# Storing the Q/K stacks of a sliding-window attention in sixteen-row blocks, with overlapping token tiles

## The chip, the cores and the metric

The kernel runs on one core of a Trainium2 chip. The metric is device time in microseconds (us), from the first to the last instruction of one execution, as the median of a few runs. The engines are PE (TensorE, with its weight-load queue PEld), DVE (VectorE), ACT (ScalarE), POOL (GpSimd) and SP (SyncE, which here issues the DMA transfers).

## The reference

A block of two parts. First comes layer norm, attention with a sliding window, the output projection and the residual; then layer norm, a gated MLP whose gate mixes the tokens (a 2048 x 2048 matrix), and the residual. Tokens S = 2048, width D = 640, 32 heads of Dh = 20. The change touches the attention:

```python
H = 32; Dh = D // H; W = 256
q, k, v = qkv[0], qkv[1], qkv[2]
scores = jnp.einsum("bhqd,bhkd->bhqk", q, k) * (Dh ** -0.5)
mask = (idx[:, None] - idx[None, :] >= 0) & (idx[:, None] - idx[None, :] < W)
scores = jnp.where(mask[None, None], scores, -1e9)
p = _softmax(scores, axis=-1)
o = jnp.einsum("bhqk,bhkd->bhqd", p, v)
```

Each query sees itself and the 255 tokens before it.

## The kernel before

**Stacks.** Q and K are wanted at fp32 accuracy from bf16 matmuls. Each is split into three bf16 parts (`split_qk`, the tile `sg`: rounding, remainder, remainder of that). A score is the sum of six products of a Q part and a K part, and all six are done in one matmul by stacking them on partitions: row 6 d + j holds dimension d of the j-th part pair, so 20 dims x 6 pairs = 120 rows. Rows 120 to 122 of the Q side hold the negated row maximum in three parts, against ones on the K side, so that the score matmul already subtracts the maximum.

A stack is for a group g of 4 heads. It lives in one of three slots (two called `slot...`, one in the storage `xb`, which earlier holds the normalized x). Each slot is two tiles, lower and upper, of [128, 2 sides, 4 heads, tokens]: tokens 0 to 1023 and 1024 to 2047. `tokens()` cuts any range of tokens that crosses 1024 into two pieces, and each piece becomes a matmul (with its weight load) of its own.

**From the Q/K GEMM to the stacks.** `qk_item(m, c)` makes 128 rows of Q/K (8 dims x 16 heads of one side or of both; m 0 to 4 are heads 0 to 15, m 5 to 9 heads 16 to 31) for the 512 tokens of chunk c, in 15 matmuls (L592 to L594). Its results are split (DVE L606, ACT L608, POOL or DVE L610, ACT L615 or POOL L613, POOL L616) and stored by one DMA on SP (L619) to the DRAM tensor `qk_d`, laid out [half of the heads, part, token half, dim of both sides, head, tokens]. `load_stack(g)` (L329) is a generator of 24 DMAs on SP: for each tile, pair j and side, 20 rows that lie six partitions apart. For the first three groups it also sets ones by a POOL memset (L322) over partitions 96 to 127.

**Order.** PE, DVE, ACT and SP follow the order of the code; POOL's order is set by a scheduler. m 0 to 5 come first (24 items, load steps of group 0 after the last four). Then `dense_tail` does m 6 to 9, interleaved with the maxima of the first 18 blocks (`LEAD`), whole 128-query matmuls on L363; the stack of group 1 is loaded from its eighth item on. The attention loop has one step s per block of 128 keys (8 groups x 16 blocks). A step issues, for each of the four heads, `max_item` for block s + 18 (L359, four strips of 32 queries, maximum on DVE L369) and `score_item` for block s (L412, four strips of 32 keys, exponential on ACT L415, masks on POOL L419 and L422), and `pv_item` for block s - 2 (L440); it also advances the load of the stack of the group after next. A max item covers its block and two before; a score item its block and the two after it, on the Q side. Both cross token 1024 in the steps 6 and 7 of each group: max blocks 8 and 9, and score blocks 6 and 7. Once in eight blocks `max_rows` transposes the maxima (L375, DVE L378 and L379, POOL L381 and L382), stores them (L384) and loads them as rows 120 to 122 (L386).

Of the kernel before, what the change touches and what calls it, by code (L numbers as in the profile page):

```python
# [34 lines left out]
def block_kernel(ctx, tc, x, xt, wqk, wv, wo, w_in, wsp, bsp, w_out, out):  # L35
# [16 lines left out]
    qk_d = dram.tile([2, 3, 2, 2 * DH, H // 2, S // 4], F32, name="qk_d")  # L52
# [203 lines left out]
    with ExitStack() as ab:  # L256
# [9 lines left out]
        s0 = [s0.tile([P, 2 * S], F32R, name=f"slot0_{i}") for i in range(2)]  # L266
# [12 lines left out]
        add_slot(2, [h[:, :2 * S] for h in xb])  # L279
# [36 lines left out]
        def load_stack(g):  # L316


            st = slot_w[g % 3]
            if g < 3:  # L320
                for h in st:
                    nc.gpsimd.memset(h[96:P, 1], ONES)  # L322
                    if g == 2:
                        yield
            for b in range(2):
                for j, parts in enumerate(((0, 0), (0, 1), (0, 2), (1, 0), (1, 1), (2, 0))):
                    for a in range(2):
                        src = qk_d[g // 4, parts[a], b, a * DH:(a + 1) * DH, g % 4 * 4:g % 4 * 4 + 4]
                        nc.sync.dma_start(st[b][j:6 * DH:6, a], src)  # L329
                        yield  # L330

        def tokens(st, rows, a, hh, t0, n):

            o = 0
            while o < n:
                c, t = divmod(t0 + o, S // 2)
                w = min(n - o, S // 2 - t)
                yield o, w, st[c][:rows, a, hh, t:t + w]
                o += w

        def one(st, rows, a, hh, t0, n):
            (_, _, x), = tokens(st, rows, a, hh, t0, n)
            return x

        def max_item(g, qb, hh, strips=True):

            st = slot_ap[g % 3]
            ps = s1_tile()
            lo = max(0, qb - 2) * P
            n = (qb + 1) * P - lo  # L350
            keep = mask[:, 384 - n:]
            if strips:
                skip = 32 if qb > 1 else 0
                if skip:
                    n, keep = 288, strip
                for j in range(4):
                    q0 = qb * P + 32 * j
                    for o, w, k in tokens(st, 120, 1, hh, lo + skip * j, n):
                        nc.tensor.matmul(ps[32 * j:32 * j + 32, o:o + w], one(st, 120, 0, hh, q0, 32), k,  # L359
                                         start=True, stop=True, tile_position=(0, 32 * j))  # L360
            else:
                for o, w, k in tokens(st, 120, 1, hh, lo, n):
                    nc.tensor.matmul(ps[:, o:o + w], one(st, 120, 0, hh, qb * P, P), k, start=True, stop=True)  # L363
            b, c = divmod(qb, 8)
            if c == 0 and hh == 0:
                m_cols[g, b] = tmp2.tile([P, 32], F32, tag="mcol", bufs=2, name=f"mcol{g}_{b}")
            junk = tmp2.tile([P, 384], BF16, tag="junk", bufs=2, name=f"junk{g}_{qb}_{hh}")
            c += hh * 8
            nc.vector.tensor_tensor_reduce(out=junk[:, :n], in0=ps[:, :n], in1=keep, scale=1.0,  # L369
                                           scalar=NEG, op0=OP.add, op1=OP.max, accum_out=m_cols[g, b][:, c:c + 1])  # L370

        def max_rows(g, b):
# [13 lines left out]
            nc.sync.dma_start(slot_w[g % 3][b][120:123, 0], rows.rearrange("a (h r) c -> a h (r c)", h=4))  # L386
# [4 lines left out]
        def score_item(u, hh):  # L391
# [14 lines left out]
            for i in range(4):  # L406
                k0 = kb * P + 32 * i
                b, e = 32 * i, min(n, 32 * i + 288)
                if NU - NT < u and 4 * (u - NU + NT - 1) + hh < 6:
                    b, e = 0, n  # L410
                for o, w, q in tokens(st, 123, 0, hh, kb * P + b, e - b):
                    nc.tensor.matmul(ps[32 * i:32 * i + 32, b + o:b + o + w], one(st, 123, 1, hh, k0, 32), q,  # L412
                                     start=True, stop=True, tile_position=(0, 32 * i))
# [51 lines left out]
        if True:  # L465
# [137 lines left out]
            def split_qk(m, c, ps):  # L603
# [10 lines left out]
                else:  # L614
                    nc.scalar.activation(sg[:, 1, :], rest, AF.Copy)  # L615
                nc.gpsimd.tensor_tensor(out=sg[:, 2, :], in0=rest, in1=sg[:, 1, :], op=OP.subtract)  # L616
                T = S // 4
                base = qk_d[m // 5, 0, c // 2, m % 5 * 8, 0, c % 2 * 256:c % 2 * 256 + 256]
                nc.sync.dma_start(bass.AP(tensor=base.tensor, offset=base.offset,  # L619
                                          ap=[[T, P], [2 * 2 * DH * H // 2 * T, 3], [1, 256]]), sg.bitcast(F32))  # L620

# [84 lines left out]
            for n in range(24):  # L706
# [11 lines left out]
                if n >= 20:  # L718
                    for _ in range(3):
                        next(ld0, None)  # L720
            def dense_tail():
                split_wqk(8)
                split_wqk(9)
                for n, (m, c) in enumerate((m, c) for c in range(4) for m in (6, 7, 8, 9)):
# [3 lines left out]
                    if n == 7:  # L728
                        x01.close()
                        s1 = pool(x01, "slot1p", side="right")  # L730
                        add_slot(1, [s1.tile([P, 2 * S], F32R, name=f"slot1_{i}") for i in range(2)])
                    if n >= 7:
                        for _ in range(3):
# [3 lines left out]
            for n in range(12):  # L737
                next(dense, None)
                if n % 5 == 4:
                    for _ in range(3):  # L740
# [12 lines left out]
            assert next(dense, 0) == 0 and next(ld0, 0) == 0  # L753
# [6 lines left out]
        for s in range(NU + 2):  # L760
            if s % NT == 0 and s < 6 * NT:
                ld = load_stack(s // NT + 2)
            for _ in range(1 + s % 2 if s >= NT else 2 * min(s, 1)):
                next(ld, None)
# [798 lines left out]
```

## Time and profile before

| | us |
|---|---|
| Runs | 1104.24, 1104.4 (median), 1109.66 |
| Profiled execution | 1106.78 |
| its span | 1105.1 |
| Q/K GEMM with the first 18 blocks' maxima, from the first max item | 178.4 to 240.4 |
| Attention steps 0 to 111 (seven groups) | 240.9 to 440.3 |
| Last group | 440.3 to about 465 |
| Projection, then the gated MLP | about 465 to the end |

The times in the profile are those of the profiled execution, counted from its first instruction. A window row gives start:end and length, and then for each engine its busy time and the number of instructions. In timeline rows the bracket at the end gives idle time of the engine before the row and what ended it; "issue" is time in which the engine waited for nothing that the profile shows. "x4" joins four instructions to one row. The granted TensorE clock is 1.00 in all windows quoted here.

### The profile page before, as it was taken

The page shows a single profiled execution, that of the slowest core. Times are in us where ns is not written, and L with a number is a line of the kernel's source. Part 1 is how long each engine was busy: PE and PEld are TensorE (multiplying, and loading weights), DVE is VectorE, ACT ScalarE, POOL GpSimd, SP SyncE. Part 2 cuts the span into 40 slices and gives each one's busy share as a digit, 9 for nine tenths or more (in the row PEclk, how much of TensorE's full clock was granted, in tenths as well). Part 3 has the DMA queues.
Part 4 walks back from the last instruction along what each step waited for, and adds up shares of the span by engine and source line. Part 5 has one row for each costly group of instructions (what it writes and reads, how often), then busy time and mean ns, then how long its engine had stood idle before and what let it go on. Part 6 is the DMA issues. An engine that isn't in the chain of part 4 may idle for free.

```text
span 1105.1 us, 28747 instructions
## 1 busy us (share of the span) xinstructions
PE 1075.2 (97%) x11059; PEld 968.4 (88%) x11059; DVE 781.0 (71%) x2157; ACT 604.7 (55%) x1258; POOL 314.0 (28%) x447
## 2 busy tenths in 40 slices
PE   8999999999999999999999999999999999999998
PEld 8998886658888787699999998999999899999998
DVE  6643445779999897575677668655556899987684
ACT  4443443249999899756766556443458433333331
POOL 4324446677766666721200012000001000000000
PEclk9999999999999999999999999999999999999999
DMA  7834657555565565689655342242441467684642
GB/s 252 296 115 118 175 172 262 169 181 171 190 188 189 178 192 151 183 263 296 252 184 174 131 142 77 66 133 97 127 148 51 173 223 254 229 276 137 195 141 96
DMA packets 92281, 194.73 MB, mean 176 GB/s; under 512 B 11952, under 2 KB 46272, under 8 KB 88256
## 3 DMA queue, kind: packets, MB, share of 16 engines
q1 hardware_dynamic: 92144, 192.90, 53.4%
q8 instruction: 87, 1.43, 0.6%
q14 instruction: 50, 0.41, 0.1%
HBM read 127.90 MB, written 64.95 MB: 175 GB/s over the span
## 4 chain that ended last, share of the span: by engine, by line
PE 79%; DMA 6%; ACT 4%; DVE 4%; issue 4%; POOL 2%; SPq 1%; DVEq 0%; POOLq 0%; ACTq 0%
PE g L1181 23%; PE pv L440 6%; PE bank L359 5%; PE bank L412 5%; PE zb L1066 4%; PE qk L592 4%; PE qk L594 4%; PE qk L593 4%; PE out_x L1345 3%; PE zx L1006 2%; PE out_v L1345 2%; PE zv L1006 2%; DMA h_d<-xh 1%; PE zy L1006 1%; PE zw L1006 1%
## 5 line engine op out<-in xcount | busy, mean ns | idle before, releaser
L415 ACT ACTIVATE pt<-bank 128x384 f32<-128x384 f32 (+1 forms) x452 | 180.2, 483 | 17.2 <-PE bank L412 10.8
L1181 PE MATMUL g<-zl,aw 128*128 128x432 f32 x768 | 169.1, 357 | 1.5 <-ACT zl L828 1.0
L369 DVE CUSTOM_DVE_ANT_0 junk<-bank,strip 128x288 bf16<-128x288 f32 x392 | 156.1, 452 | 12.3 <-PE bank L359 10.1
L828 ACT ACTIVATE aw<-fx 128x512 fp32r<-128x512 f32 (+2 forms) x152 | 86.2, 587 | 127.6 <-DVE fx L822 57.9
L1181 PEld LDWEIGHTS g<-zl,aw 128*128 128x128 f32 x768 | 144.0, 188 | 8.1 <-ACT zl L828 1.4
L440 PE MATMUL pv<-pt,v_sb 128*32 128x192 f32 (+3 forms) x1984 | 135.2, 322 | 4.6 <-POOL pt L419 2.4
L822 DVE TENSOR_TENSOR aw<-fx,aw 128x512 fp32r<-128x512 f32 (+2 forms) x152 | 95.8, 638 | 60.1 <-ACT aw L828 59.8
L1181 PE MATMUL g<-ze,aw 128*128 128x432 f32 x576 | 132.6, 359 | 2.3 <-DVE row L822 2.3
L1181 PEld LDWEIGHTS g<-ze,aw 128*128 128x128 f32 x576 | 107.1, 188 | 9.0 <-DVE row L822 3.7
L419 POOL TENSOR_SCALAR_AFFINE_SELECT pt<-pt 128x512 f32<-128x512 f32 x128 | 83.5, 653 | 61.2 <-ACT pt L415 59.0
L412 PE MATMUL bank<-slot 123*32 123x288 bf16 (+8 forms) x1296 | 95.7, 273 | 2.0 <-issue 1.3
L359 PE MATMUL bank<-slot 120*32 120x288 bf16 (+6 forms) x1248 | 93.5, 275 | 0.9 <-DVE mcol L369 0.8
L440 PEld LDWEIGHTS pv<-pt,v_sb 128*32 128x32 f32 x1984 | 65.5, 110 | 11.9 <-POOL pt L419 6.2
L422 POOL TENSOR_SCALAR_AFFINE_SELECT pt<-pt 128x512 f32<-128x512 f32 x112 | 71.2, 635 | 0.0
L412 PEld LDWEIGHTS <-slot 123*32 123x32 bf16 x1728 | 58.8, 96 | 13.0 <-issue 3.6
L359 PEld LDWEIGHTS <-slot 120*32 120x32 bf16 x1408 | 52.1, 95 | 15.2 <-issue 7.2
L369 DVE CUSTOM_DVE_ANT_0 junk<-bank,mask 128x384 bf16<-128x384 f32 (+2 forms) x120 | 51.2, 444 | 17.0 <-PE bank L363 15.7
L822 DVE TENSOR_TENSOR row<-g,row 128x432 f32<-128x432 f32 x80 | 48.3, 603 | 21.0 <-PE g L1181 20.6
L616 POOL TENSOR_TENSOR sg<-rest,sg 128x512 bf16<-128x512 f32 x40 | 46.7, 1167 | 56.3 <-ACT sg L615 45.6
L606 DVE TENSOR_TENSOR rest<-qk,std 128x512 f32<-128x512 f32 x40 | 27.6, 690 | 44.9 <-PE qk L594 44.9
L608 ACT ACTIVATE sg<-rest 128x512 bf16<-128x512 f32 x40 | 25.2, 631 | 54.3 <-DVE rest L606 54.3
L118 PE MATMUL wo_ps<-xb,xb 128*128 128x320 f32 x260 | 52.4, 311 | 1.5 <-DVE mvc L1460 1.5
(263 smaller groups left out, 2538.4 us busy)
## 6 DMA issues: line engine op xcount, KB each, us to landing
slot<-qk_d SPq DMA_DIRECT2D x144, 160.0 KB
fx<-wsp_in SPq DMA_DIRECT2D x32, 512.0 KB
qk_d<-sg SPq DMA_DIRECT2D x40, 384.0 KB
o_d<-ot SPq DMA_DIRECT2D x64, 128.0 KB
xb<-qk_d SPq DMA_DIRECT2D x48, 160.0 KB
fx<-hn_d SPq DMA_DIRECT2D x24, 320.0 KB
z_d<-row SPq DMA_DIRECT2D x16, 432.0 KB
g_d<-row SPq DMA_DIRECT2D x16, 432.0 KB
```

What stands on the lines that cost most here:

```text
L359: nc.tensor.matmul(ps[32 * j:32 * j + 32, o:o + w], one(st, 120, 0, hh, q0, 32), k, start=True, stop=True, tile_position=(0, 32 * j))
L369: nc.vector.tensor_tensor_reduce(out=junk[:, :n], in0=ps[:, :n], in1=keep, scale=1.0, scalar=NEG, op0=OP.add, op1=OP.max, accum_out=m_cols ...
L412: nc.tensor.matmul(ps[32 * i:32 * i + 32, b + o:b + o + w], one(st, 123, 1, hh, k0, 32), q, start=True, stop=True, tile_position=(0, 32 * i))
L415: nc.scalar.activation(pt[:, hh, :n], ps[:, :n], AF.Exp, scale=SCALE)
L419: nc.gpsimd.affine_select(out=pt[:, :, :P], in_=pt[:, :, :P], pattern=[[0, 4], [1, P]], base=0, channel_multiplier=-1, compare_op=OP.is_ge ...
L422: nc.gpsimd.affine_select(out=pt[:, :, 256:], in_=pt[:, :, 256:], pattern=[[0, 4], [-1, P]], base=-1, channel_multiplier=1, compare_op=OP. ...
L440: nc.tensor.matmul(ps[32 * hh:32 * hh + 32, a - 512 * c:b - 512 * c], v_sb[:, kb, v0:v0 + 32], pt[:, hh, a - kb * P:b - kb * P], start=fir ...
L822: (eng or nc.vector).tensor_tensor(out=out, in0=a, in1=b, op=op)
L828: nc.scalar.activation(out, a, AF.Copy)
L1006: nc.tensor.matmul(ps, a[x], b[:, y], start=start and m + x + y == 0, stop=stop and m == n - 1 and x == 1, skip_group_check=True)
L1181: nc.tensor.matmul(ps, w[m][:, x, k], zc[k][m][:, y], start=start and k + x + y == 0, stop=stop and k == 3 and x == 1, skip_group_check=True)
L1345: nc.tensor.matmul(o[b][:, :HD], l[:, x, k * P:(k + 1) * P], r[k][:, y], start=start and k + x + y == 0, stop=stop and k == 2 and x == 1, ...
```

## The change

The stack's rows are in another order, and its tiles are cut elsewhere.

- Row 7 d + j now holds dimension d below 16 of pair j, at 0 to 5 of each seven rows (partitions j, j + 7, ... j + 105). The last four dims of all pairs fill what is left: the sixteen rows 6, 13, ... 111 and rows 112 to 119.
- The upper tile holds tokens 768 to 2047 (n = 640 words of two tokens), the lower one still 0 to 1023. Max blocks from 8 on and score blocks from 6 on read the upper tile, so no range is ever cut and `tokens()` is gone.
- In DRAM there is a `qk_d` for each tile (16 dims) and a `qr_d` for each tile, which holds the last four dims once for each of the six pairs. A Q/K item is stored for each tile that it lies in, with one DMA, and the items of m 4 and 9, which hold the last dims, with three for each side and tile. The stores repeat a part that several pairs use. Stores rise from 40 to 100.
- A stack takes 32 loads: for each tile 12 of 16 rows, two of 16 rows and two of 8. The rows of the maxima for blocks 0 to 7 go to both tiles (three loads a group, no longer two).
- `load_stack` is stepped four times where it was three, and twice a step in the attention loop.
- The Q/K weights are permuted ahead of the launch, so that m 4 and 9 are the last dims of both sides.

```diff
+    WORDS = (S // 4, S // 4 + P)
+    qk_d = [dram.tile([2, 2, 3, 16, H // 2, n], F32, name=f"qk_d{b}") for b, n in enumerate(WORDS)]
+    qr_d = [dram.tile([2, 2, 6, DH - 16, H // 2, n], F32, name=f"qr_d{b}") for b, n in enumerate(WORDS)]
+    PAIRS = ((1, 0), (0, 1), (0, 0), (0, 2), (2, 0), (1, 1))
...
-                        src = qk_d[g // 4, parts[a], b, a * DH:(a + 1) * DH, g % 4 * 4:g % 4 * 4 + 4]
-                        nc.sync.dma_start(st[b][j:6 * DH:6, a], src)
+                        nc.sync.dma_start(st[b][j:j + 106:7, a], qk_d[b][q, a, parts[a], :, heads])
                         yield
+                for a in range(2):
+                    last = qr_d[b][q, a, :, :, heads].rearrange("j d h t -> (j d) h t")
+                    nc.sync.dma_start(st[b][6:112:7, a], last[:16])
+                    yield
+                    nc.sync.dma_start(st[b][112:6 * DH, a], last[16:])
+                    yield
...
+        def one(st, b, rows, a, hh, t0, n):
+            t = t0 - 6 * P * b
+            return st[b][:rows, a, hh, t:t + n]
...
+            half_b = qb // 8
...
-                    for o, w, k in tokens(st, 120, 1, hh, lo + skip * j, n):
-                        nc.tensor.matmul(ps[32 * j:32 * j + 32, o:o + w], one(st, 120, 0, hh, q0, 32), k,
-                                         start=True, stop=True, tile_position=(0, 32 * j))
+                    nc.tensor.matmul(ps[32 * j:32 * j + 32, :n], one(st, half_b, 120, 0, hh, q0, 32),
+                                     one(st, half_b, 120, 1, hh, lo + skip * j, n),
+                                     start=True, stop=True, tile_position=(0, 32 * j))
...
+            if b == 0:
+                nc.sync.dma_start(st[0][120:123, 0], rows)
+                nc.sync.dma_start(st[1][120:123, 0, :, :P], rows[:, :, 6 * P // 2:])
+            else:
+                nc.sync.dma_start(st[1][120:123, 0, :, P:], rows)
...
+                    for a in range(2):
+                        for p in range(3):
+                            js = [j for j, x in enumerate(PAIRS) if x[a] == p]
+                            base = qr_d[b][m // 5, a, js[0], 0, 0, o:o + t1 - t0]
+                            step = (js[-1] - js[0]) // max(1, len(js) - 1)
+                            nc.sync.dma_start(bass.AP(tensor=base.tensor, offset=base.offset,
+                                                      ap=[[W, 64], [4 * n * W * step, len(js)], [1, t1 - t0]]),
+                                              part[64 * a:64 * a + 64, p:p + 1].to_broadcast([64, len(js), t1 - t0]))
...
-            for _ in range(1 + s % 2 if s >= NT else 2 * min(s, 1)):
+            for _ in range(2 if s >= NT else 2 + (s % 3 == 1) if s else 0):
```

What it does to the order, at three places. On PE, a max item of block 8 and the head of the score item behind it, in the attention loop; `bank` is a PSUM bank, `slot_0` and `slot_1` the lower and upper tile. Before:

```order
L440 MATMUL pv_1_4650<-pt_4549,v_sb 32x256 x4
L359 LDWEIGHTS slot_1_103
L359 MATMUL bank_121<-slot_0_102,slot_1_103 32x256
L359 LDWEIGHTS slot_1_103
L359 MATMUL bank_121<-slot_1_103 32x32
L359 LDWEIGHTS slot_1_103
L359 MATMUL bank_121<-slot_0_102,slot_1_103 32x224
L359 LDWEIGHTS slot_1_103
L359 MATMUL bank_121<-slot_1_103 32x64
```

The same place after:

```order
L447 MATMUL pv_1_4615<-pt_4689,v_sb 32x256 x4
L359 LDWEIGHTS slot_1_106
L359 MATMUL bank_122<-slot_1_106 32x288
L359 LDWEIGHTS slot_1_106
L359 MATMUL bank_122<-slot_1_106 32x288
L359 LDWEIGHTS slot_1_106
L359 MATMUL bank_122<-slot_1_106 32x288
L359 LDWEIGHTS slot_1_106
L359 MATMUL bank_122<-slot_1_106 32x288
```

Each strip is one matmul of 288 columns in place of two. The order of the items is the same; 488 matmuls and 488 weight loads are gone from the whole program.

On SP, the stores of two Q/K items and the first loads of group 0's lower tile, in the first loop (`sg` are the split results). Before:

```order
L619 DMA qk_d<-sg_1_1520 128x3x256
L586 DMA std_3_1551<-rstd_d 128x512
L556 DMA wqraw_1553<-wqk_in 128x640
L619 DMA qk_d<-sg_1_1548 128x3x256
L329 DMA slot_0_102<-qk_d 20x2048 x3
```

The same place after:

```order
L641 DMA qr_d_66<-sg_1_1532 64x3x256
L641 DMA qr_d_66<-sg_1_1532 64x2x256
L641 DMA qr_d_66<-sg_1_1532 64x256
L641 DMA qr_d_66<-sg_1_1532 64x3x256
L641 DMA qr_d_66<-sg_1_1532 64x2x256
L641 DMA qr_d_66<-sg_1_1532 64x256
L641 DMA qr_d_67<-sg_1_1532 64x3x128
L641 DMA qr_d_67<-sg_1_1532 64x2x128
L641 DMA qr_d_67<-sg_1_1532 64x128
L641 DMA qr_d_67<-sg_1_1532 64x3x128
L641 DMA qr_d_67<-sg_1_1532 64x2x128
L641 DMA qr_d_67<-sg_1_1532 64x128
```
```order
L593 DMA std_3_1574<-rstd_d 128x512
L563 DMA wqraw_1576<-wqk_in 128x640
L633 DMA qk_d_64<-sg_1_1571 128x3x256
L633 DMA qk_d_65<-sg_1_1571 128x3x128
L332 DMA slot_0_105<-qk_d_64 16x2048 x4
```

The store of item (4, 1) has become twelve, that of (5, 1) two, and four loads follow where three did. All stand in one queue.

On POOL, the end of the Q/K GEMM, where `xb` gets its ones for the third slot. Before:

```order
L381 CAST m_0_1_2321<-mr_1_2322 32x128
L382 TENSOR_TENSOR m_0_1_2321<-mr_1_2322,m_0_1_2321 32x128
L616 TENSOR_TENSOR sg_3_2292<-rest_3_2293,sg_3_2292 128x512
L322 MEMSET xb_98 32x2048
L610 TENSOR_TENSOR rest_3_2344<-rest_3_2344,sg_3_2343 128x512
```

After:

```order
L382 CAST m_0_1_2388<-mr_1_2389 32x128
L325 MEMSET xb_101 32x2560
L383 TENSOR_TENSOR m_0_1_2388<-mr_1_2389,m_0_1_2388 32x128
L623 TENSOR_TENSOR sg_3_2358<-rest_3_2359,sg_3_2358 128x512
L617 TENSOR_TENSOR rest_3_2411<-rest_3_2411,sg_3_2410 128x512
```

The memset is a quarter longer, and it has moved two instructions ahead. Behind it stand the last splits of the Q/K GEMM and the first mask of the attention loop.

More of the change, by code (lines that the diff above doesn't have):

```diff
@@ L265, in block_kernel @@
         s0 = pool(low0, "slot0p")
-        s0 = [s0.tile([P, 2 * S], F32R, name=f"slot0_{i}") for i in range(2)]
+        s0 = [s0.tile([P, 8 * n], F32R, name=f"slot0_{i}") for i, n in enumerate(WORDS)]
         xn = [h.rearrange("p (a k t) -> p a k t", a=2, k=KD) for h in (xa[:, :CH], xa[:, CH:], *xb)]
@@ L278, in block_kernel @@
         add_slot(0, s0)
-        add_slot(2, [h[:, :2 * S] for h in xb])
+        add_slot(2, [h[:, :8 * n] for h, n in zip(xb, WORDS)])
         mask = tmp2.tile([P, 384], BF16, name="mask")
@@ L357, in max_item @@
                     q0 = qb * P + 32 * j
[L358 to L363 removed]
+                    nc.tensor.matmul(ps[32 * j:32 * j + 32, :n], one(st, half_b, 120, 0, hh, q0, 32),
+                                     one(st, half_b, 120, 1, hh, lo + skip * j, n),
+                                     start=True, stop=True, tile_position=(0, 32 * j))
+            else:
+                nc.tensor.matmul(ps[:, :n], one(st, half_b, 120, 0, hh, qb * P, P), one(st, half_b, 120, 1, hh, lo, n),
+                                 start=True, stop=True)
             b, c = divmod(qb, 8)
@@ L410, in score_item @@
                     b, e = 0, n
-                for o, w, q in tokens(st, 123, 0, hh, kb * P + b, e - b):
-                    nc.tensor.matmul(ps[32 * i:32 * i + 32, b + o:b + o + w], one(st, 123, 1, hh, k0, 32), q,
-                                     start=True, stop=True, tile_position=(0, 32 * i))
+                c = int(kb > 5)
+                nc.tensor.matmul(ps[32 * i:32 * i + 32, b:e], one(st, c, 123, 1, hh, k0, 32),
+                                 one(st, c, 123, 0, hh, kb * P + b, e - b),
+                                 start=True, stop=True, tile_position=(0, 32 * i))
             if u <= NU - NT:
@@ L718, in block_kernel @@
                 if n >= 20:
-                    for _ in range(3):
+                    for _ in range(4):
                         next(ld0, None)
@@ L730, in dense_tail @@
                         s1 = pool(x01, "slot1p", side="right")
-                        add_slot(1, [s1.tile([P, 2 * S], F32R, name=f"slot1_{i}") for i in range(2)])
+                        add_slot(1, [s1.tile([P, 8 * n], F32R, name=f"slot1_{i}") for i, n in enumerate(WORDS)])
                     if n >= 7:
-                        for _ in range(3):
+                        for _ in range(4):
                             next(ld1, None)
@@ L739, in block_kernel @@
                 if n % 5 == 4:
-                    for _ in range(3):
+                    for _ in range(4):
                         next(ld0, None)
@@ L752, in block_kernel @@
                     next(rows)
-            assert next(dense, 0) == 0 and next(ld0, 0) == 0
+            assert next(dense, 0) == 0 and next(ld0, 0) == 0 and next(ld1, 0) == 0
             for _ in after[0]:
```

37 lines of the change are left out of this document (19 added, 18 removed).

## The prediction

> **What bounds the kernel now.** I read the page's first part, then the attention stage group by group (240.9 to 440.3 us, sixteen steps a group), since every matmul that the change takes away is there.
>
> ```profile
> PE 1075.2 (97%) x11059; PEld 968.4 (88%) x11059; DVE 781.0 (71%) x2157; ACT 604.7 (55%) x1258; POOL 314.0 (28%) x447
> ```
>
> TensorE is the bound over the whole. By windows (start:end, length, busy time and instructions of each engine), two of the seven groups:
>
> ```profile
> 353.95:383.88 29.93, 27.50 (x836) 23.43 (x832) 26.58 (x137) 26.16 (x68) 19.59 (x35) 1.00 0.56 178
> 383.88:411.32 27.44, 27.23 (x835) 23.02 (x831) 26.58 (x137) 26.10 (x69) 19.59 (x35) 1.00 0.61 195
> ```
>
> The same work takes 27.4 us in one group and 29.9 in its neighbour, with the same 26.6 us of VectorE and the clock at 1.00. So something stops the engines that is no operand. Cut into four steps each, steps 6 to 9 of the seven groups stand first below; the last row is four steps elsewhere:
>
> ```profile
> 252.17:259.71 7.54, 7.25 (x251) 6.40 (x245) 7.20 (x36) 6.95 (x18) 5.54 (x11) 1.00 0.57 180
> 279.69:287.47 7.78, 7.42 (x254) 6.28 (x250) 7.33 (x36) 6.96 (x18) 5.58 (x11) 1.00 0.65 220
> 307.28:315.72 8.44, 7.46 (x255) 6.73 (x250) 7.20 (x36) 7.11 (x19) 5.75 (x11) 1.00 0.65 201
> 335.60:344.23 8.63, 7.38 (x252) 6.36 (x246) 7.22 (x36) 6.94 (x19) 5.56 (x11) 1.00 0.60 197
> 364.04:374.09 10.05, 7.78 (x255) 6.75 (x250) 7.12 (x36) 7.12 (x19) 6.71 (x12) 1.00 0.52 169
> 393.97:401.32 7.35, 7.33 (x252) 6.17 (x245) 7.03 (x36) 6.88 (x18) 5.54 (x11) 1.00 0.61 196
> 422.20:431.11 8.91, 7.78 (x256) 6.63 (x249) 7.20 (x36) 7.07 (x18) 6.32 (x12) 1.00 0.48 138
> 300.45:307.28 6.83, 6.83 (x217) 6.00 (x214) 6.57 (x34) 6.74 (x18) 4.89 (x8) 1.00 0.47 139
> ```
>
> The excess sits in steps 6 to 9, from 7.35 to 10.05 us for equal work: 58.70 us together. Steps 6 and 7 are where blocks cross token 1024 and each matmul is issued in two pieces (some 250 matmuls recorded in the four steps, not 217). The chain of waits names the stop (start, length, what):
>
> ```profile
> 309.70 0.98 issue
> ...
> 340.24 1.06 issue
> ...
> 366.46 1.21 issue
> ...
> 372.02 1.07 issue
> ...
> 424.64 0.88 issue
> ```
>
> These are 5.2 us in which TensorE waited for nothing that the profile shows, all in those windows. What they wait for shows in two rows of TensorE's timeline elsewhere, two of the split step, and the end of a stop:
>
> ```profile
> 300.76 0.31 PE L359 MATMUL bank<-slot 120*32 120x288 bf16 x4
> 300.89 0.31 PE L412 MATMUL bank<-xb 123*32 123x288 bf16 x4
> ...
> 306.62 0.27 PE L359 MATMUL bank<-slot,slot 120*32 120x256 bf16 x4
> ...
> 306.75 0.27 PE L412 MATMUL bank<-xb 123*32 123x256 bf16 x4
> ...
> 310.69 0.20 PE L359 MATMUL bank<-slot,slot 120*32 120x64 bf16 x2 [0.98 <-issue]
> ```
>
> An item of four whole matmuls occupies TensorE for 0.13 us (300.76 to 300.89); one of eight half matmuls also for 0.13 (306.62 to 306.75). So the pieces cost nothing while they run: the price comes some 3 us later, as a stop. The queue that carries instructions has this row (packets, MB, share):
>
> ```profile
> q8 instruction: 87, 1.43, 0.6%
> ```
>
> 1.43 MB over 2 x 11059 TensorE instructions is 65 bytes each, and over 87 packets some 254 instructions a packet. A step with whole matmuls issues 96 of them ((836 - 64) / 16 matmuls and as many weight loads) in about 1.7 us, a split step 160. My reading, an inference: TensorE runs ahead of the packets in two split steps, and stops until the next one has come.
>
> **The change part by part.**
>
> *Matmuls.* 488 of them go, with 488 weight loads: 64 a group in steps 6 and 7. Directly this is worth nothing, by the 0.13 us above. If the stops go, steps 6 to 9 fall to the next bound. That isn't 6.8 us, because they carry extra VectorE work: VectorE is busy 7.03 to 7.33 us in those windows against 6.57, and the group without a stop took 7.35. I take 7.25, just under that group: 58.70 - 7 x 7.25 = 8.0 us gained. Bounds: 5.2 (only the named stops) and 11.1 (58.70 - 7 x 6.8); zero if the stops have another cause.
>
> *Loads and stores on SP.* The rows (minimum, median, maximum ns; first and last start):
>
> ```profile
> L329 SPq DMA_DIRECT2D slot<-qk_d x144: 694/703/1202, 160.5 to 412.3; - x144
> L619 SPq DMA_DIRECT2D qk_d<-sg x40: 359/366/422, 93.4 to 244.7; - x40
> L511 SPq DMA_DIRECT2D rstd_d<-std_row x1: 338/338/338, 74.2 to 74.2; - x1
> L386 SPq DMA_DIRECT2D slot<-m_d x12: 262/269/364, 217.8 to 442.8; - x12
> ```
>
> Stores rise from 40 to 100, loads from 24 to 32 a group, but a load has 16 or 8 rows, no longer 20. No row shows a strided 16-row load or the repeated store. The nearest are the 16-row transfer (0.34), the three-row one (0.27) and the present store (0.37); the far end is the 20-row load's 0.70. I take 0.37 for both, as the row count is nearest. In attention this makes SP lighter (two loads a step at 0.37 against one and a half at 0.70), so nothing is lost there. The tight place is before the first max item, where SP is nearly full and TensorE waits for the last lower-tile load:
>
> ```profile
> 157.04 0.36 SPq L619 DMA_DIRECT2D qk_d<-sg  x1
> 157.50 0.43 SPq L586 DMA_DIRECT2D std<-rstd_d  x1
> ...
> 171.05 2.20 SPq L329 DMA_DIRECT2D slot<-qk_d x3
> ```
> ```profile
> 178.42 0.22 PE L363 MATMUL bank<-slot 120*128 120x128 bf16 x1 [0.15 <-DMA slot<-qk_d]
> ```
>
> The twelve loads that it needs are issued by 173.25, and it already waits for data, so there is no slack. After the change 157.04 begins with twelve stores in place of one, and up to the sixteenth load SP issues 27 stores, 16 loads and four other transfers of about 0.5 (0.43 for the one above): 43 x 0.37 + 4 x 0.5 = 17.9, so 175.0 without any wait, 1.8 later. If the data then lands as late after its issue as now, TensorE loses 1.8; if the smaller loads land sooner by as much, nothing. I take 0.4, near the lower end: now the data comes only some 5 us after 173.25, while a lone transfer needs about 2 (next fence). Bounds: -0.2 (even the present wait goes) and, at 0.70 a piece, 1.8 + 43 x 0.33 = 16.0.
>
> The upper tile has the same edge at 206, where the first matmul that reads both tiles starts:
>
> ```profile
> 199.56 0.73 SPq L329 DMA_DIRECT2D slot<-qk_d  x1
> ...
> 203.49 0.37 SPq L619 DMA_DIRECT2D qk_d<-sg  x1
> ```
> ```profile
> 206.02 0.28 PE L363 MATMUL bank<-slot,slot 120*128 120x256 bf16 x1
> ```
> ```profile
> 443.66 1.94 DMA o_d<-ot
> ```
>
> Now the twelfth load of that tile is issued at 199.56, ahead of the store at 203.49. After the change there are sixteen, and the last stands behind that store, which is now two, so it starts at 204.3. With 0.37 to issue and 1.94 to land that is 206.6, for a matmul whose weights are wanted at 205.9: +0.7, at 5 us of landing +3.8. I take 0.9.
>
> [...]
>
> *GpSimd.* The ones are now set in 2560 columns instead of 2048, and the order puts that memset directly ahead of the operation at 238.16, no longer behind the subtraction at 238.55. Its chain, and the TensorE row it ends in:
>
> ```profile
> 238.16 0.42 POOL L382 TENSOR_TENSOR m<-mr,m 32x128 bf16<-32x128 f32 x1
> 238.55 1.15 POOL L616 TENSOR_TENSOR sg<-rest,sg 128x512 bf16<-128x512 f32 x1
> 239.75 1.80 POOL L322 MEMSET xb<- 32x2048 f32 x1
> ...
> 244.66 0.65 POOL L419 TENSOR_SCALAR_AFFINE_SELECT pt<-pt 128x512 f32<-128x512 f32 x1
> ```
> ```profile
> 245.36 0.53 PE L440 MATMUL pv<-pt,v_sb 128*32 128x192 f32 x8 [0.95 <-POOL pt L419]
> ```
>
> GpSimd works almost without a gap from 238.16 to the mask at 244.66, and TensorE waits 0.95 us for it, so nothing covers a longer memset: 1.80 x 2560/2048 = 2.25, +0.45. The memset's storage is also read by the Q/K matmuls, of which this is the last:
>
> ```profile
> 238.45 0.40 PE L594 MATMUL qk<-xb,wql 128*128 128x512 f32 x1
> ```
>
> So the moved memset can start at 238.85 at the earliest, no longer hidden behind the subtraction, and GpSimd idles from 238.16 for 0.7 us more: +1.15. If instead the scheduler's place costs nothing, only 0.45 is left. I take 0.9 between the two; nothing in it can gain.
>
> *Sum.* Profiled execution 1106.78 - 8.0 + 0.4 + 0.9 + 0.9 = 1101.0. The median of the runs, 1104.4, lies 2.4 below the profiled execution, so 1098.6.
>
> **The rivals.**
>
> *The stops stay (same).* The stops may belong to the mere number of packets, which falls from 87 by only 4 (976/254), or to data transfers that hold a packet up; against the latter, the worst window (10.05) has a low DMA share, 0.52. For it: one group has all its splits and no stop (393.97). Then only the costs are left, 2.2, less 7 x 0.1 for that group's 7.35 against 7.25: 1104.4 + 1.5 = 1105.9.
>
> [...]
>
> *SP becomes the bound before the first max item (slower).* One mechanism: a small strided load or a repeated store costs SP nearer the 0.70 us of the 20-row load than 0.37. At a price p the loads are late by 1.8 + 43 (p - 0.37) us and TensorE stands at 178 for as long; that eats the other terms, 8.0 - 0.9 - 0.9 = 6.2, from p = 0.47 on. At 0.65 it is 13.8: 1104.4 - 6.2 + 13.8 = 1112.0. For it: the one price that the trace has for a load from this tensor. Against it: three rows of 0.27 to 0.37.
>
> *All the excess goes (faster still).* The windows fall to 6.8 us, VectorE's extra work being absorbed by the steps around: 11.1 instead of 8.0, no cost by SP's loads, 0.45 on GpSimd: 1104.4 - 10.65 = 1093.8. Against it: VectorE is busy 26.58 of the best group's 27.44 us, so the steps around have little room.
>
> **How the numbers follow.** Forecast 0.64, stops stay 0.16, SP late 0.11, all goes 0.09. Half a per cent, 5.5 us, is about what a measurement of this kernel can tell from no change: faster means under 1098.9, slower over 1109.9. The forecast's own range is 1095 to 1102, by gains of 5.2 to 9.8 and costs of 0.4 to 2.8; 0.37 of its 0.64 lies under 1098.9. With the case in which all goes, faster is 0.46. SP late gives 0.08 beyond the slower bound and 0.03 within it; 0.04 more is for stops that move to other steps and grow: slower 0.12. The rest, 0.42, is no change. The range of 8 in 10 reaches from 1092.5 to 1106.5, so that it holds the rival in which the stops stay.
>
> **What would show it.** In the profile after: no issue pieces over 0.5 us in the chain in steps 6 to 9, those windows all at 7.1 to 7.4 us, groups at 27.0 to 27.4; new 16-row loads at 0.34 to 0.40 us on SP and the repeated stores alike; TensorE's waits for loads near 178 and 206 us below 2 us each; GpSimd's first mask 0.45 to 1.15 us later against the end of the Q/K work. Wrong would be: stops of about 1 us at other steps, loads at 0.6 us or more, or steps 6 to 9 that stay above 7.8 without any issue piece.

## The result and the profile after

The changed kernel takes 1148.01 us (median of 6 runs, 1146.09 to 1151.14) against 1106.2 us for the kernel before in the same comparison: 1.038 of it, 95% interval 1.0357 to 1.0403. It is slower by 42 us, where 5.8 us less had been forecast (1098.6 against 1104.4). Ratios leave out runs that are over 1.5% above the fastest of their kernel, medians count all. The profiled execution has a span of 1149.4 us, 44.3 more than before.

The stages, by the same marks in both profiles, tell where the 44 us are:

| | before | after | more |
|---|---|---|---|
| start of the first max item | 178.42 | 190.37 | +12.0 |
| from there to the first exponential of the attention loop | 62.5 | 66.6 | +4.1 |
| attention, groups 0 to 6 | 199.4 | 227.5 | +28.1 |
| from there to the end | 664.8 | 664.9 | +0.1 |

The first part of the page shows that VectorE, ScalarE and GpSimd have as much to do as before. TensorE has 488 instructions fewer and a lower share, though it is busy 11 us longer; part of its work now runs at a lower clock, as shown below:

```profile
PE 1086.4 (95%) x10571; PEld 970.8 (84%) x10571; DVE 783.3 (68%) x2157; ACT 605.0 (53%) x1258; POOL 315.3 (27%) x447
```

**The steps of the split blocks.** Windows over steps 6 to 9 of groups 0 and 1, and over the whole of group 3 (columns as in the prediction):

```profile
270.64:277.75 7.11, 7.03 (x202) 5.91 (x194) 7.02 (x36) 6.90 (x18) 5.54 (x11) 1.00 0.61 173
301.76:308.84 7.08, 7.08 (x202) 6.03 (x201) 6.95 (x34) 6.80 (x17) 4.42 (x9) 1.00 0.64 190
353.39:386.98 33.59, 28.20 (x772) 23.68 (x768) 26.88 (x137) 26.08 (x69) 19.68 (x35) 0.95 0.60 171
```

Steps 6 to 9 take 7.1 us here, with 202 matmuls for 250, and the stops on "issue" are gone from them. (So they do in group 5; in the others, where TensorE has just stood for a load, they take 8.1 to 8.7.) But group 3 takes 33.6 us for work that keeps VectorE busy for 26.9.

**The new stops in attention.** TensorE's timeline at group 3's steps 5 and 6, and its longest waits for transfers over the attention loop (us, times, longest; the rows of the weight loads between them are left out):

```profile
367.20 0.31 PE L359 MATMUL bank<-slot 120*32 120x288 bf16 x4 [4.19 <-DMA slot<-qr_d]
368.54 0.43 PE L418 MATMUL bank<-slot 123*32 123x288 bf16 x4 [1.04 <-DMA slot<-m_d]
```
```profile
PE bank L359 <- DMA slot<-qr_d: 10.3, 4, 4.2
PE bank L359 <- DMA o_d<-ot: 4.2, 2, 2.8
PE bank L359 <- DMA xb<-qr_d: 4.2, 1, 4.2
PE bank L418 <- DMA slot<-m_d: 3.1, 3, 1.7
```

(A step is counted here from its first exponential to the next step's, so a stop ahead of step 6's first max item falls to step 5.) The max item of block 8, the first to read the next group's upper tile, waits for the last loads of that stack. The program puts those loads some seven steps ahead of it. SP's timeline has the last two of them at

```profile
362.99 0.49 SPq L336 DMA_DIRECT2D slot<-qr_d  x1
363.53 0.47 SPq L338 DMA_DIRECT2D slot<-qr_d  x1
```

TensorE has stood since 363.0 (367.20 less 4.19), when SP had not yet issued the last one; it goes on 3.2 us after that. So SP runs late in its own order. How late shows in the store of the maxima, which follows TensorE's transpose of them by way of VectorE and GpSimd. After and before, transpose and store:

```profile
334.35 0.42 PE L376 MATMUL bank<-ident,mcol 128*32 128x128 f32 x1
```
```profile
344.35 0.34 SPq L385 DMA_DIRECT2D m_d<-m  x1
```
```profile
322.36 0.27 PE L375 MATMUL bank<-ident,mcol 128*32 128x128 f32 x1
```
```profile
325.20 0.40 SPq L384 DMA_DIRECT2D m_d<-m  x1
```

SP is 10.0 us behind the transpose after the change, and was 2.8 us behind it before.

**The prices on SP.** Rows by tile (minimum, median, maximum ns; first and last start):

```profile
L332 SPq DMA_DIRECT2D slot<-qk_d x144: 484/587/1785, 166.4 to 457.1; - x144
L336 SPq DMA_DIRECT2D slot<-qr_d x24: 484/493/1122, 185.0 to 461.2; - x24
L338 SPq DMA_DIRECT2D slot<-qr_d x24: 471/478/932, 185.7 to 461.8; - x24
L641 SPq DMA_DIRECT2D qr_d<-sg x60: 468/602/1445, 146.7 to 263.5; - x60
L390 SPq DMA_DIRECT2D slot<-m_d x6: 762/767/845, 238.3 to 473.4; - x6
```

A load of sixteen rows costs 0.59 us, one of eight 0.48, a repeated store 0.60, and the load of maxima into part of a tile's columns 0.77. In a group that is 24 x 0.587 + 8 x 0.485 = 18.0 us for the stack, against 24 x 0.703 = 16.9 before; 1.3 more for the maxima (0.24 + 0.77 + 0.77 against 2 x 0.27 before, and a third gap); and the output's stores cost 0.525 in place of 0.413 (medians of L469 and L462, eight a group), 0.9 more. With the stores of maxima (2 x 0.34), some 0.06 us between 45 transfers, and two waits between the store and the load of maxima (1.8 us each on average, at most 3.5), that makes 31 to 34 us. Groups 1 to 6 take 31 to 34.5.

SP's own timeline shows it without medians. Of the 33.2 us that groups 1 to 5 take on average, its transfers take 27.0, gaps of under 0.15 us between them 2.6, and longer waits 3.6, all but 0.1 of these ahead of the loads of the maxima. So SP is never early enough to wait for any other result, and its work is what a group takes. Before the change it was 23.0, 2.2 and 3.2 of 28.4 us: there was little room there either.

**Ahead of the first max item.** SP's timeline, and TensorE's:

```profile
154.12 10.04 SPq L641 DMA_DIRECT2D qr_d<-sg  x12
...
166.37 3.08 SPq L332 DMA_DIRECT2D slot<-qk_d  x4
...
186.79 0.48 SPq L338 DMA_DIRECT2D slot<-qr_d  x1
```
```profile
181.48 0.77 PE L599 MATMUL qk<-xa,wqh 128*128 128x512 f32 x1 [4.35 <-DVE rest L613]
...
190.37 0.27 PE L363 MATMUL bank<-slot 120*128 120x128 bf16 x1 [5.99 <-DMA slot<-qr_d]
```

The last of the sixteen loads is issued at 187.3, not at the 175.0 of the prediction. (The 10.04 us of the x12 row include 1.7 us in which SP stands between its stores.) TensorE stands twice: first for a split that waits (as I read it, for one of three buffers that the late stores still hold), then for the data. The windows that follow (the column behind POOL is the granted clock) show a second price, a lower clock behind these stops:

```profile
190.00:194.00 4.00, 3.63 (x11) 2.35 (x11) 0.89 (x6) 0.00 (x0) 0.79 (x1) 0.52 1.04 328
194.00:198.00 4.00, 4.00 (x21) 2.45 (x20) 2.19 (x11) 1.13 (x2) 1.16 (x1) 1.00 1.05 374
```

For about four more microseconds TensorE works at half its clock (0.52 in the first window), which costs it about 1.9 us by my estimate (4.00 x 0.48). Together with a stop of 2.58 us at 222.27 that covers the second row of the table (4.1 us). The clock is lower behind stops in attention too; first the window behind the one that ends at 367.2, then step 2 of group 0, where TensorE stands 1.84 us for GpSimd's first mask:

```profile
367.20:373.00 5.80, 4.76 (x94) 4.04 (x98) 3.67 (x16) 2.67 (x7) 1.62 (x4) 0.71 0.60 172
260.17:265.32 5.15, 3.31 (x56) 2.00 (x55) 2.14 (x11) 1.86 (x5) 4.35 (x7) 0.68 0.83 212
```

Not every stop has that behind it: after the 5.99, the 4.19 and the 1.84 us above the windows show 0.52, 0.71 and 0.68, after the 2.58 us at 222.27 the clock stays at 1.00 (222.27 to 226.27). What decides it, no run here takes apart.

### The profile page after: what moved, and what is told of

The parts are those of the page before. It is cut to its first block, busy times and chain, and to the rows that moved or that the text cites. A ratio compares the mean times of both kernels' runs of the same rounds, so it can differ in the third digit from the quotient of the medians.

```text
span 1149.4 us, 27970 instructions
## 1 busy us (share of the span) xinstructions
PE 1086.4 (95%) x10571; PEld 970.8 (84%) x10571; DVE 783.3 (68%) x2157; ACT 605.0 (53%) x1258; POOL 315.3 (27%) x447
## 4 chain that ended last, share of the span: by engine, by line
PE 55%; issue 17%; DMA 9%; ACT 6%; SPq 5%; DVE 4%; POOL 3%; POOLq 0%; DVEq 0%; ACTq 0%
PE g L1205 11%; PE pv L447 4%; PE zb L1090 4%; PE bank L359 3%; PE bank L418 3%; PE out_x L1369 3%; ACT pt L422 3%; PE qk L599 3%; PE qk L601 3%; PE qk L600 3%; PE zx L1030 2%; SPq L641 2%; DMA m_d<-m 2%; DMA xh<-x_in 2%; PE out_v L1369 2%
## 5 line engine op out<-in xcount | busy, mean ns | idle before, releaser
L447 PE MATMUL pv<-pt,v_sb 128*32 128x192 f32 (+3 forms) x1984 | 137.5, 329 | 4.4 <-POOL pt L426 3.1
L359 PE MATMUL bank<-slot 120*32 120x288 bf16 (+2 forms) x1248 | 96.8, 292 | 15.6 <-DMA slot<-qr_d 10.3
L418 PE MATMUL bank<-slot 123*32 123x288 bf16 (+7 forms) x1296 | 98.0, 289 | 4.1 <-DMA slot<-m_d 3.1
L359 PEld LDWEIGHTS <-slot 120*32 120x32 bf16 x1248 | 47.3, 97 | 29.8 <-DMA slot<-qr_d 8.6
L418 PEld LDWEIGHTS <-slot 123*32 123x32 bf16 x1536 | 53.4, 98 | 17.4 <-DMA slot<-m_d 3.8
```

The costliest lines, as they stand in the source:

```text
L359: nc.tensor.matmul(ps[32 * j:32 * j + 32, :n], one(st, half_b, 120, 0, hh, q0, 32), one(st, half_b, 120, 1, hh, lo + skip * j, n), start=T ...
L418: nc.tensor.matmul(ps[32 * i:32 * i + 32, b:e], one(st, c, 123, 1, hh, k0, 32), one(st, c, 123, 0, hh, kb * P + b, e - b), start=True, sto ...
L447: nc.tensor.matmul(ps[32 * hh:32 * hh + 32, a - 512 * c:b - 512 * c], v_sb[:, kb, v0:v0 + 32], pt[:, hh, a - kb * P:b - kb * P], start=fir ...
```

## The experiments

Each run is compared with the kernel before on the same chip (four chips, on which that takes 1103.2 to 1105.2 us). A time without a ratio is of a single execution; the changed kernel's six spread by 5 us, so less than that says little there. "Later" means one edit, which several runs share:

```diff
-                if hh == 3 and u1 % 8 == 1 and s <= NU - LEAD + 1:
+                if hh == 3 and u1 % 8 == 3 and 19 < u1 <= NU + 3:
                     next(rows)
```

It puts the load of the maxima two steps behind its place. Theory 1 is that SP's queue is what is late; the rivals blame the transfers, the new tiles or the new layout in DRAM.

### One part alone: the token tiles, and the pieces put back

The first kernel takes only the upper tile from token 768, with the old stack (24 loads of 20 rows six apart). The second does the same and still issues the crossing strips in two pieces, now out of one tile.

```diff
-        s0 = [s0.tile([P, 2 * S], F32R, name=f"slot0_{i}") for i in range(2)]
+        s0 = [s0.tile([P, 8 * n], F32R, name=f"slot0_{i}") for i, n in enumerate(WORDS)]
...
+        def pieces(t0, n):                     # the second kernel only
+            w = S // 2 - t0
+            return ((0, w), (w, n - w)) if 0 < w < n else ((0, n),)
```

> Only the token half of the change: upper tile from token 768, whole matmuls; the stacks stay 24 loads of 20 rows six apart, the stores one per item and tile (50, no longer 40). Theory 1 (the loss is SP's queue, and the gain from whole matmuls is there underneath): the issue stops in steps 6 to 9 are gone, those steps take about 7.1 us as in the changed kernel's first groups, 58.7 - 7 x 7.1 = 9 us gained, less about 1 us for the longer memset: 0.992 of before, 1098. Rival (the upper tile's larger transfers, 200 KB for 160, or the later start of the data is what is slow): TensorE waits for loads at step 6 of each group, over 1115.

> As the run before, but the strips of the blocks that cross token 1024 are still issued in two pieces, from one tile. If the stops come from the number of TensorE instructions in two steps (160 a step for 96), they are back: 1105 to 1107, with issue pieces of about 1 us after steps 6 and 7. If they come from reading two tiles or from something else that the new tiles change, it is as fast as the run before.

Measured: 1115.7 us, ratio 1.0084 (1.0055 to 1.0114), and 1115.75 us, ratio 1.0097 (1.0068 to 1.0125). Theory 1's 1098 is missed by far, and the rival's "over 1115" is met. That the pieces cost nothing here would be the second branch of the second expectation, but the two kernels lose their time in different places: TensorE stands 7.9 us on "issue" with the pieces and 4.3 without, and 0.5 us for loads with them and 7.5 without. The next section compares them with SP relieved. In the profile of the first, steps 6 to 9 take 7.08 to 7.30 us in six groups and 8.30 in one, as the forecast said for whole matmuls; but in groups 3 to 6 step 5 takes 1.2 to 3.8 us more than its usual 1.76, the longest like this:

```profile
340.24 0.31 PE L351 MATMUL bank<-slot 120*32 120x288 bf16 x4 [3.01 <-DMA xb<-qk_d]
340.90 0.43 PE L410 MATMUL bank<-slot 123*32 123x288 bf16 x4 [0.36 <-DMA slot<-m_d]
```

The same stop as in the changed kernel, with the old loads. Whether SP's queue is late or the 200 KB transfers are, this run doesn't tell. On SP hardly anything but the loads of maxima has changed in attention, 0.27 and twice 0.74 us for twice 0.27, some 1.3 us a group with the gap.

### The load of the maxima two steps later

> The changed kernel, with the load of the row maxima put two steps later in the program, so that SP no longer stands 2 to 3 us twice a group between their store and their load. Theory 1 (SP's queue holds up attention: some 28 us of issue and 5 us of that wait in a group of 33 us): groups 1 to 6 fall from 31 to 34.5 us to 28 to 30, some 20 us in all: 1125 to 1130. Rival (the transfers themselves are late, whatever SP does): no change, 1146 to 1151.

> Token tiles alone (24 loads of 20 rows), with the load of the row maxima two steps later. If what ate the gain of that kernel is SP's queue (three loads of maxima at 0.27, 0.74 and 0.74 us for two at 0.27, and a wait between their store and their load twice a group, so that the stack's last loads come some microseconds late at step 5), then the stops at step 5 go: attention 191 to 194 us for 209, the whole 1097 to 1100, 0.993 to 0.996 of before. Rival (the 200 KB transfers are late by themselves): 1112 to 1118 as without the shift.

> As the run before, with the crossing strips in two pieces. With SP out of the way, the price of the pieces should show: if the instruction stream limits them, 7 to 10 us slower than the run before, with issue pieces of about 1 us in steps 6 to 9; if the pieces are free, equal within 2 us.

> The kernel before, with the load of the row maxima two steps later. If SP is not what binds the kernel before (its stops are instructions), no change: within 2 us of before. If its queue already sets part of the group's time, 5 to 10 us faster.

The changed kernel with the edit takes 1135.02 us, 13 less than without, and its attention 211.6 us for 227.5: the direction of theory 1, two thirds of the size (1125 to 1130 had been expected). Group 6, during which SP has no stack to load, takes 27.2 us; groups 1, 3 and 5 still take 31 to 32, and in them SP issues 47 to 50 transfers, for 28 to 29.5 us, without any idle time but the short gaps.

The token tiles with the edit take 1105.69 us, ratio 1.0008 (0.9995 to 1.002): 10 us less than without it, which the rival excludes (the transfers are the same), but not faster than before, so theory 1's 1097 to 1100 is missed too. Its attention takes 195.5 us, and SP has hardly any idle time left in groups 3 to 5 (0 to 0.4 us). With the pieces: 1110.7 us, 1.0044 (1.0023 to 1.0065). The kernel before with the edit: 1103.24 us, 0.9993 (0.9976 to 1.0011), no change, the first of its two branches: there the edit only leaves SP 3 to 5 us a group in which it waits for other engines. So the pieces cost 4 (by the ratios) to 5 us (by the medians) where SP has its waits taken away, under the 7 to 10 expected; the two intervals are barely apart. Their waits in attention, pieces first (that profile is of the slowest of its ten runs, 1114.75 us):

```profile
PE bank L416 <- issue: 7.5, 8, 1.8
PE bank L356 <- issue: 2.7, 3, 1.0
```
```profile
PE pv L439 <- POOL pt L418: 1.9, 1, 1.9
PE pv L439 <- issue: 1.9, 1, 1.9
```

10.2 us of stops on "issue" with the pieces, 1.9 without, and both read a single tile: the stops come with the pieces, so with the number of instructions, and not with reading two tiles.

### Ahead of the first max item

> The changed kernel, with the 60 repeated stores of the last dims issued by ScalarE, not SP. Theory 1 (27 stores at 0.6 us each stand ahead of the first max item's loads on SP): the first max item starts at about 180 us, not 190, the waits for the loads between 177 and 260 are mostly gone, attention is as slow as in the changed kernel: 1130 to 1136. Rival (the repeated stores' bytes in the DMA engines are what delays the loads): the first max item stays at about 190, 1148.

```diff
-                            nc.sync.dma_start(bass.AP(tensor=base.tensor, offset=base.offset,
+                            nc.scalar.dma_start(bass.AP(tensor=base.tensor, offset=base.offset,
```

Measured: 1162.12 us, worse, and the first max item at 192.2. This tested nothing of what it was made for: a store costs ScalarE 0.61 us too, and six of them (6.78 us with the waits, from 179.03) stand in front of the rounding that the next Q/K item waits for (TensorE: 5.07 us "<-ACT sg L622" at 189.5). I had left out what was behind them on that engine.

> The changed kernel with the maxima's load two steps later, and with the weight columns permuted so that the last dims of heads 0 to 15 are item m = 0 and not m = 4: their 30 stores stand on SP between 90 and 130 us, where it waits for the splits, and not ahead of the first max item. Theory 1 (27 stores of 0.6 us in SP's queue make the first max item 12 us late): it starts at 178 to 180 us and not 189.6, and the whole is 11 to 14 us faster than that kernel's 1135: 1121 to 1124. Rival (the repeated stores' or loads' bytes, or the new load form by itself, are late): it stays at 185 or later, over 1130.

```diff
-                    if m % 5 < 4:
+                    if m not in (0, 9):
```

Measured: the first max item at 178.7, as theory 1 says and its rival excludes, with the same bytes and the same loads. The attention loop starts 10.8 us earlier (245.25 for 256.09). The whole is 1128.81, only 6 us less than 1135, where 1121 to 1124 had been expected: attention took 216.7 us for 211.6. One profile of each doesn't tell whether these 5 us are due to the edit.

> The kernel before, with each of the 40 stores of Q/K split into three (one for each part; same bytes). It measures the price of a store in a burst. If a store costs 0.37 wherever it stands, the second and third cost 0.37 and the first max item's loads are at most 2 us later. If only a store that finds SP idle costs 0.37, the second and third cost 0.5 to 0.6 us, and the first max item starts 3 to 6 us later than 178.

Measured: 1105.25 us, and the first max item at 178.8. A store of 128 rows costs 0.40 us (median) behind another transfer and 0.32 behind idle time, so both prices are off, but the first expectation's consequence holds (at most 2 us later; it is 0.4): a burst is not what makes a store dear. The 0.60 belongs to the repeated 64-row form.

### Fewer and more transfers on SP

> The changed kernel with the maxima's load two steps later, and without the eight loads of last rows for groups 3 to 7 (left out: the last four dims of these groups' stacks are stale, those of an earlier group). Theory 1: SP is relieved of 8 x 0.53 = 4.3 us in a group, the stops at step 5 go in groups 2 to 6 (31.1, 29.3, 32.0, 29.2, 32.3 us there in that kernel, to about 27.3): 15 to 18 us off 1135: 1117 to 1120. Rival (a stop at step 5 is the landing of a large transfer, not SP's lag): the last load is then one of the 160 KB loads, and the stops stay: 1130 to 1136.

> The kernel before (tiles at 1024, no repeated stores), with each 20-row load issued as one of 16 rows and one of 4: the same bytes, twice the DMAs on SP. Theory 1 (SP's issue time alone): 24 x 0.63 + 24 x 0.5 + some 11 us for the rest = 38 us of SP in a group whose work takes 27.4: groups 1 to 6 take 34 to 38 us, attention 240 to 260, the whole 1145 to 1165. Rival (the loss in the changed kernel comes from its new layout in DRAM and its rows seven apart): under 1115.

```diff
-                        nc.sync.dma_start(st[b][j:6 * DH:6, a], src)
+                        nc.sync.dma_start(st[b][j:j + 91:6, a], src[:16])
+                        nc.sync.dma_start(st[b][j + 96:6 * DH:6, a], src[16:])
```

Without the eight loads of last rows the kernel takes 1121.67 us, 13 less than 1135 and just over the 1117 to 1120 of theory 1. Three of the five groups concerned:

```profile
319.90:346.81 26.91, 26.67 (x772) 22.32 (x768) 26.37 (x137) 25.89 (x69) 19.58 (x35) 1.00 0.59 172
374.15:401.02 26.87, 26.63 (x772) 22.43 (x768) 26.41 (x137) 25.88 (x68) 19.56 (x35) 1.00 0.58 169
401.02:427.91 26.89, 26.66 (x772) 22.31 (x768) 26.47 (x137) 25.90 (x68) 19.58 (x35) 1.00 0.63 177
```

26.9 us each, 27.3 and 27.9 in the other two: with room on SP the whole matmuls bring what was forecast, and 7.1 us in steps 6 to 9. Group 1, which still waits for the full stack of group 2, takes 34.9.

With the loads of the kernel before cut in two, same tiles, same layout, same bytes: 1151.87 us, near the middle of what theory 1 gave and far from the rival's "under 1115", and attention 244.7. Its SP rows and one group:

```profile
L329 SPq DMA_DIRECT2D slot<-qk_d x144: 496/507/2147, 160.2 to 465.7; - x144
L330 SPq DMA_DIRECT2D slot<-qk_d x144: 586/587/890, 160.8 to 466.2; - x144
```
```profile
416.79:453.62 36.83, 28.96 (x836) 24.14 (x832) 27.06 (x137) 26.17 (x69) 19.72 (x35) 0.91 0.49 141
```

The number of transfers on SP alone makes the kernel before as slow as the change did, while the data moves slower than before (141 GB/s for 178 and 195 in the two groups of the prediction). Here too SP has next to no idle time in groups 1 to 5 but the short gaps. The price doesn't follow the rows: here four rows cost more (0.587) than sixteen (0.507). Part of it comes from the transfer ahead: each load of four rows stands behind one of sixteen, and the output's stores cost 0.32 us (median) behind idle time, 0.43 behind a 20-row load in the kernel before and 0.53 behind a sixteen-row load in the changed one.

### Towards a faster version

> The candidate: token tiles alone with 20-row loads, maxima's load two steps later, the ones of the slots 1 and 2 copied by DMA from slot 0's in place of memsets on GpSimd, and the first group's loads begun one item earlier. If GpSimd's memset ahead of the first mask costs what step 2 of group 0 shows (3.8 us for 1.5) and the rest stays as in the kernel without the copies, 2 to 3 us faster than that one and 1 to 4 us faster than before: 0.996 to 0.999. If the copies only lengthen SP's queue: 1.001 to 1.003.

```diff
-                    nc.gpsimd.memset(h[96:P, 1], ONES)
+                    if g:
+                        nc.sync.dma_start(h[120:123, 1], h0[120:123, 1])
+                    else:
+                        nc.gpsimd.memset(h[96:P, 1], ONES)
```

Measured: 1101.2 us for 1103.16, ratio 0.9989 (0.9965 to 1.0012): inside the expected range, and not to be told from no change. Step 2 of group 0 takes 2.07 us where it took 3.8 with the memset, so that part is shown.

> As the candidate with copied ones, but the stack is ordered by pairs (20 rows of one pair behind the other, pairs in an order in which the parts of both sides run on), so that 12 loads of 60, 40 or 20 rows do what 24 of 20 rows did. Theory 1 (SP's queue, at 27 us a group beside work of 26.9, is what hides the whole matmuls' gain): SP falls to some 18 to 20 us a group, no stop at step 5 is left, groups take 26.9 to 27.3 us, attention 188 to 191: 1094 to 1097, 0.990 to 0.994 of before. Rival (whole matmuls bring less than their 9 us, or loads of 480 KB land late and take it back): 1100 to 1106 as the kernels with 24 loads.

> As the run before, with the crossing strips issued in two pieces each: the price of the 488 extra matmuls and weight loads with SP out of the way. If they cost what the stops in the kernel before show: 6 to 9 us slower than the run before. If they cost nothing without SP's lag: equal within 2 us.

```diff
+                for j, n in ((0, 3), (3, 2), (5, 1)):
+                    for a in range(2):
+                        i = (3 - n) * a
+                        src = qk_d[b][q, a, i:i + n, :, heads].rearrange("i d h t -> (i d) h t")
+                        nc.sync.dma_start(st[b][j * DH:(j + n) * DH, a], src)
```

Measured: 1157.99 us (1142.54 to 1166.66), ratio 1.0424 (1.0366 to 1.0483), and with the pieces 1157.25 us (1155.09 to 1165.59), 1.0469 (1.0425 to 1.0513). The first is far off both its branches. That the two agree within 2 us is no answer on the price of the pieces, with such a spread. The profile of the first is of its fastest run. It is 43 us longer than the candidate's, 13 of them ahead of the attention loop, which nothing here takes apart, and 30 in it. SP is free now, at 0.37 us a load:

```profile
L335 SPq DMA_DIRECT2D slot<-qk_d x72: 272/368/1067, 161.8 to 449.8; - x72
```

No load is waited for in attention; but the stops on "issue" are back, and longer, without a single crossing strip:

```profile
PE bank L356 <- issue: 20.9, 6, 4.1
```

Six groups of seven stop at step 11, by 2.7 to 4.1 us, amid loads of 160 to 600 KB. Around one such stop (TensorE resumes at 313.37 after 3.21 us), the transfers from 302.6 to 310.6 and from 310.6 to 313 (queue: packets, MB, share of 16 engines):

```profile
q1 hardware_dynamic: 426, 1.46, 81.1%
```
```profile
q1 hardware_dynamic: 256, 0.52, 77.5%
q8 instruction: 1, 0.02, 3.4%
```

For eight microseconds no packet of instructions arrives on q8 while data takes 81% of the DMA engines' time; then one comes (at 310.69), and TensorE goes on 2.7 us later. This is no single case. The kernel before has five stops of TensorE on "issue" of over 0.8 us in attention, and each ends 2.2 to 3.2 us after a packet on q8 began; packets come every 4.4 us there (median), at most 5.8 us apart, and the stop here follows a gap of over 8 us. I read the stops as waits for instructions, as the prediction did; the traces show the times and not the cause. That data of large loads is what delays the packets is my reading too, and no run here shows it.

## Why the prediction was wrong

- **Whole matmuls gain 8.0 us: mechanism right, gain hidden.** Steps 6 to 9 fell to 7.1 us (7.25 forecast) where no load was late, and groups with room on SP to 26.9. From the 58.70 us of those windows that is 9.0. In the changed kernel the late loads stop the same steps. In whole runs the pieces cost 4 to 5 us (1110.7 against 1105.69). The rival in which the stops stay is out.
- **"I take 0.37 for both, as the row count is nearest": the step that failed.** The stores cost 0.60, the loads 0.59 and 0.48, which the prediction had named as a sign of being wrong. The rows that I took the price from have other forms: one plain store of 128 rows and lone small transfers. The far end of my bounds, the 20-row load's 0.70 from the same tensor, was the better guide.
- **Ahead of the first max item** the slower rival came as written: 1.8 + 43 (p - 0.37) gives 11.7 us at p = 0.60, and 12.0 were measured. The mechanism is right; that the numbers agree so closely is luck. SP began this stretch 2.9 us earlier than the formula has it (154.12, not 157.04), stood or paused 4.7 us that it left out, and the data landed sooner: the item starts 3.1 us after the last issue, 5.2 before. The rival had been given 0.11. With the stores moved away the item started at 178.7 again.
- **"In attention this makes SP lighter, so nothing is lost there": wrong, and two thirds of the loss.** I had counted only the loads, and not the load of maxima into both tiles (0.77 twice), the wait between store and load, and that the kernel before needed some 26 us of SP in a group of 28 (16.9 for the stack, 3.3 for the output, 1.3 for the maxima, some 2 for gaps and 2 to 3 for the waits). So 1.1 us more for the stack, 1.3 for the maxima and 0.9 for the output were enough to make SP the bound. The rival was placed at 178 us alone, so even its 1112 stayed 36 us short.
- **The upper tile's edge at 206:** 0.9 forecast, 2.58 measured (at 222.3, "<-DMA slot<-qr_d"), by the same price.
- **GpSimd's memset:** 0.9 forecast; TensorE waits 1.84 us for the mask, 0.95 before. Right: the memset waited 0.66 us for the last Q/K matmul and took 2.23. But the step with that wait took 5.15 us for 2.92 before, with the clock at 0.68 in it; with the tiles alone, where the clock stayed at 1.00, it took 3.8.
- **The clock** had no term. Behind the stops of 5.99, 4.19 and 1.84 us it was 0.52, 0.71 and 0.68, over windows of 4.00, 5.80 and 5.15 us: by my estimate (window times what is missing to 1.00) 1.9, 1.7 and 1.6 us more.

What stays open: what sets the price of one transfer on SP (four rows at 0.587, 20 to 60 at a median of 0.37), what makes the instruction packets late, and whether a stack can be loaded with few transfers on SP and without large bursts, so that the 9 us show in a whole kernel.

## What to carry to other kernels

An engine that only issues transfers can be the bound though no busy row says so (here SP's transfers, gaps and waits took 27.0, 2.6 and 3.6 us of the 33.2 us of a group): add up its issue times, the gaps and the waits that it stands in, per period of the loop, and compare the sum with the period before adding to it. Take a transfer's price from a row of the same form and tensor, and where there is none, let the dearest row of the same tensor weigh in the forecast and not only in the range. How late such a queue runs is read from one transfer whose cause is known, such as the store of a result against the instruction that made it.

## What the runs showed that I had not expected

- SP's price per transfer goes by its form and by the transfer ahead of it: 0.32 to 0.40 us for a 128-row store of Q/K, 0.59 for sixteen rows seven apart behind another such load and 0.49 behind a store, 0.51 for sixteen rows six apart, 0.59 for four rows six apart behind those, 0.60 for a repeated 64-row store, 0.77 for three rows in part of their columns, 0.37 (median) for 20 to 60 adjacent rows.
- With 12 larger loads a stack in place of 24, TensorE stopped up to 4.1 us for no operand, 20.9 us in attention, with 81% of the DMA engines' time taken ahead of one such stop. That stop ends 2.7 us after an instruction packet begins, the five of over 0.8 us in the kernel before 2.2 to 3.2 us after one.
